# Keys through the DMA crossbar, and batch 0's queries split by token, in a fused pooling-attention and maxout feed-forward kernel

## Chip, cores, metric

One core of one Trainium2 chip. Times are device microseconds (us) of one execution, medians of the runs of a kernel; kernels that are compared ran on the same chip. Ratios are the mean time of one kernel's fast runs over that of the other's fast runs of the same rounds, so they are not quite the ratio of the medians that stand beside them.

## The reference

```python
# B, H, S, D = 8, 8, 576, 64; pool = 8, so 72 pooled keys and values per head
k_p, v_p = mean of k, v over groups of 8 tokens
attn = softmax(q @ k_p.T / 8)                  # 576 x 72 per head
x = (attn @ v_p), heads side by side           # 4608 tokens x 512
h = max(max(x @ w1, x @ w2), x @ w3)           # 4608 x 768
out = h @ w_out                                # 4608 x 512, float32
```

## The kernel before

The feed-forward runs in nine blocks of 512 tokens. In each block TensorE's stream is a list of groups: 18 hidden groups of four 512-column matmuls (six column slices of the hidden layer, three weights each), then 4 projections. Behind a group the plan puts pieces of the attention of the batch that comes next: `s0` to `s7` the scores of a head, `v0` to `v4` the values of a token chunk, `x0` to `x4` that chunk's transpose, `T` the next batch's query transpose, `k` its keys. Block 0 and all before it, the head, have a plan of their own.

Tiles lie in one of two on-chip memories: SBUF, into which the loads go, and PSUM, which TensorE writes its results to. The pooled keys of a batch lie as 96 rows of 6 x 128. They are transposed, and copied into a key matrix `kz` of two halves, one for even and one for odd token positions (`par`). The scores of every head need both halves.

```python
def keys(b, tag):                                   # six transposes on TensorE, into PSUM
    pkt = psp.tile([128, 6, 96], BF16, name="pkt", ...)
    for i in range(6):
        nc.tensor.transpose(pkt[:, i, :], kps[b][:, i, :, :], ident[0:96, 0:96])
    return pkt

def fill_kz(b, par, h0, h1, pkt, evac):
    rows = slice(64 * par, 64 * par + 64)
    evac(out=kz_all[b % 2][rows, par, h0:h1, 0:Sp].rearrange("p h (r i) -> p h r i", i=6),
         in_=pkt[rows, :, 12 * h0:12 * h1].rearrange("p i (h r) -> p h r i", r=12))

def turn_k(b):
    pkt = keys(b, TR)
    for par in range(2):
        fill_kz(b, par, 0, H, pkt, nc.scalar.copy if b == 1 else nc.vector.tensor_copy)
...
# head: loads of batch 0 in this order
load_k(0, ((2, 4), (4, 6)));  load_q(0, 0, 2);  load_q(0, 2, 4);  load_v(0, (0, 4, 6, 8))
...
def plan(n):                                        # blocks 1 to 8; a number is a group of the block
    b, i = n + 1, 3 * (n == 1)
    got = {0: [], 3: [], 3 + i: [(b, "k")]}
    got.update({5 + i + h: [(b, f"s{h}")] for h in range(H)})
    got[12 + i].append((b + 1, "T"))
    got.update({15 + i + c: [(b, f"v{c} x{c}")] for c in range(5)})
```

`fill_kz` copies from PSUM. How long one such copy takes (min/median/max, in ns, with the first and last start and the shapes):

```profile
L179 ACT COPY kz<-pkt x4: 393/513/634, 10.2 to 30.9; 64x288 bf16<-64x288 bf16 x2, 64x576 bf16<-64x576 bf16 x2
```

The softmax here doesn't subtract the row's maximum and nothing guards it: scores larger than these inputs give would overflow.

Of the kernel before, what the change touches and what calls it, by code (L numbers as in the profile page):

```python
# [14 lines left out]
def kernel(  # L15
# [11 lines left out]
    nc = tc.nc  # L27
# [11 lines left out]



    NG = 9
    GS = (0, 2, 4, 6, 8, 1, 3, 5, 7)
    NR = 64
    KCH = C // 128
    JCH = DFF // 128
# [8 lines left out]
    psp = ctx.enter_context(tc.tile_pool(name="psp", bufs=1, space=PSUM))  # L55
    ctx.enter_context(tc.manual_schedule())

    kts, vts, qbs, kps, qTs, ets = {}, {}, {}, {}, {}, {}

    def after(loads, first):  # L60
        for x in loads:
# [16 lines left out]
        for h, g in zip(cuts, cuts[1:]):  # L78
            nc.gpsimd.dma_start(out=vts[b][:, h:g], in_=src[:, h:g])  # L79

    def load_q(b, i=0, j=4):
        if b not in qbs:
            qbs[b] = ld.tile([128, 4, NG, D], BF16, name="qb", tag="qb")
        src = q[b].rearrange("h s d -> (h s d)").rearrange(
            "(hp p t d) -> p hp t d", hp=4, p=128, t=NG)
        nc.gpsimd.dma_start(out=qbs[b][:, i:j], in_=src[:, i:j])

    w_sb = [const.tile([128, KCH, DFF], F16, name=f"mw{wi}", tag=f"mw{wi}")
            for wi in range(3)]
# [9 lines left out]
    kt0 = const.tile([96, 2, POOL, D], F32, name="kt0", tag="kt0")  # L99
    nc.sync.dma_start(out=kt0, in_=rows_k(0)[:, 0:2])  # L100
    load_k(0, ((2, 4), (4, 6)))
    load_q(0, 0, 2)
    load_q(0, 2, 4)
    load_v(0, (0, 4, 6, 8))
    warm = const.tile([128, 512], BF16, name="warm", tag="warm")
    nc.vector.memset(warm, 1.0)
    ident = const.tile([128, 128], BF16, name="ident", tag="ident")
# [52 lines left out]
    def turn_q(b, n0, n1, evac, tag):  # L160
        if b not in qTs:
            qTs[b] = sb2.tile([128, 2 * NG, 128], BF16, name="qT", tag="qT")
        pqt = psp.tile([128, n1 - n0, 128], BF16, name="pqt", tag=tag[0],
                       bufs=tag[1])
        qf = qbs[b].rearrange("p hp t d -> p (hp t d)")
        for n in range(n0, n1):
            nc.tensor.transpose(pqt[:, n - n0, :], qf[:, 128 * n:128 * n + 128],  # L167
                                ident)
        evac(out=qTs[b][:, n0:n1, :], in_=pqt)

# [10 lines left out]
             in_=pkt[rows, :, 12 * h0:12 * h1].rearrange("p i (h r) -> p h r i", r=12))  # L181

    def turn_k(b):
        pkt = keys(b, TR)
        for par in range(2):
            fill_kz(b, par, 0, H, pkt,
                    nc.scalar.copy if b == 1 else nc.vector.tensor_copy)

    def pool_k(b, tag):

# [8 lines left out]
    def score(b, h, out, tp, i0, i1):  # L199

        f = NG * (h // 2) + tp
        n = f // 2
        nc.tensor.matmul(out, kz_all[b % 2][:, f % 2, h, :],  # L203
                         qTs[b][:, n + i0:n + i1, 64 * (h % 2):64 * (h % 2) + 64],
                         start=True, stop=True)

    def exp(out, in_):
# [45 lines left out]
    PW = ("pw", 3)  # L253

    QS = ((0, 5), (5, 10), (10, 14), (14, 18))
    xns, mms = {}, []

    def do(b, steps):




        for name in steps.split():
            i = int(name[1:] or 0)
            if name[0] in "qQ":
                turn_q(b, *QS[i], nc.vector.tensor_copy if name[0] == "Q"
                       else nc.scalar.copy, TR)
            elif name[0] == "T":
                qTs[b] = sb2.tile([128, 2 * NG, 128], BF16, name="qT", tag="qT")
                nc.sync.dma_start_transpose(  # L270
                    out=qTs[b], in_=qbs[b].rearrange("p hp t d -> p (hp t d)"))
            elif name[0] == "k":
                turn_k(b)
            elif name[0] == "K":
                pool_k(b, PW)
            elif name[0] == "a":
                nc.vector.tensor_tensor(out=k16, in0=kts[b][:, :, 0:4],
                                        in1=kts[b][:, :, 4:8], op=ALU.add)
            elif name[0] == "s":
                if i == 0:  # L280
                    new_et(b)
                scores(b, i)
            elif name[0] == "v":
                xns[b, i] = values(b, CHUNKS[i][0])
            else:
                turn_x(b, *CHUNKS[i], xns[b, i], TR,
                       nc.vector.tensor_copy if name[0] == "X" else nc.scalar.copy)

    def hidden_part(n, jc, c0, c1, hT):
        col = slice(NB * n + c0, NB * n + c1)  # L290
        t = None
        for wi in range(3):
            pw = psp.tile([128, c1 - c0], F32, name=f"pw{wi}", tag="pw", bufs=3)
            for kc in range(KCH):
                mm = nc.tensor.matmul(pw, w_sb[wi][:, kc, bass.ts(jc, 128)],  # L295
                                 xT[:, kc, col],
                                 start=(kc == 0), stop=(kc == KCH - 1))
            mms.append(mm)
            if wi == 0:
                t = sb2.tile([128, c1 - c0], F16, name="t0", tag="t0")  # L300
                nc.scalar.copy(out=t, in_=pw)  # L301
            elif wi == 1:
                t1 = sb2.tile([128, c1 - c0], F16, name="t1", tag="t1")
                nc.vector.tensor_tensor(out=t1, in0=t, in1=pw, op=ALU.max)  # L304
                t = t1
            else:
                nc.vector.tensor_tensor(out=hT[:, jc, c0:c1], in0=t, in1=pw,  # L307
                                        op=ALU.max)
            yield

    def hidden(n, hT):

        parts = [(0, JCH, 0, NB)]
        if n == 0:
            parts = [(0, 1, 0, 128), (0, 1, 128, 256), (1, 2, 0, 256), (0, 2, 256, NB),
                     (2, JCH, 0, NB)]
        elif n == 1:
            parts = [(0, 1, 0, 256), (0, 1, 256, NB), (1, JCH, 0, NB)]
        for j0, j1, c0, c1 in parts:
            for jc in range(j0, j1):  # L320
                yield from hidden_part(n, jc, c0, c1, hT)

    def project(n, hT):
        for mm in range(4):
# [3 lines left out]
            for c in ((slice(0, C // 2), slice(C // 2, C)) if last else (slice(0, C),)):  # L328
# [8 lines left out]
                for u in range(2):  # L337
                    b, g = divmod(2 * m + u, NG)
                    dst = out[S * b:S * b + S, :].rearrange("(r g) c -> r g c", g=NG)
                    (nc.scalar if last and u else nc.sync).dma_start(  # L340
                        out=dst[:, GS[g], c], in_=osb[64 * u:64 * u + 64, c])
            yield

    def new_hT():
# [5 lines left out]
    def heat(n):  # L350
        for _ in range(n):
            nc.tensor.matmul(wm, warm[:, 0:128], warm, start=True, stop=True)
# [6 lines left out]
    for i in range(0, 6, 2):  # L359
# [7 lines left out]
            out=kps[0][:, i:i + 2].rearrange("p i a d -> p a i d"),  # L367
            in0=f[:, None, :, 0].to_broadcast([96, 2, 2, D]),
            in1=f[:, None, :, 1].to_broadcast([96, 2, 2, D]), op=ALU.add)
    turn_q(0, 0, 5, nc.vector.tensor_copy, PW)  # L370
    turn_q(0, 5, 9, nc.scalar.copy, ATT)
    pkt0 = [keys(0, PW) for _ in range(2)]
    for h in (0, 4):
        fill_kz(0, 0, h, h + 4, pkt0[0], nc.vector.tensor_copy)
        fill_kz(0, 1, h, h + 4, pkt0[1], nc.scalar.copy)

    def scores4(h):
        psc = psp.tile([128, 4, 256], F32, name="psc4", tag="att", bufs=2)
        for i in range(4):
            score(0, h + i, psc[:, i, :], 0, 0, 4)  # L380
        exp(ets[0][:, h:h + 4, 0:256], psc[0:Sp])

    def scores2(h):
        psc = psp.tile([128, 2, 512], F32, name="psc2", tag="att", bufs=2)
        for i in range(2):
            score(0, h + i, psc[:, i, 0:64], 0, 4, 5)
            score(0, h + i, psc[:, i, 64:320], 1, 0, 4)
        exp(ets[0][:, h:h + 2, 256:S], psc[0:Sp, :, 0:320])

    def first_values():  # L390
# [11 lines left out]
                out=xns[0, 0][:, g], in0=pav[:, :, 0:D],  # L402
                in1=rcp.to_broadcast([128, 4, D]), op=ALU.mult)

    def first_turn(g, tag):
        pxt = psp.tile([128, 2, 128], F16, name="pxt0", tag=tag[0], bufs=tag[1])
        for kc in range(2):
            nc.tensor.transpose(pxt[:, kc, :],
                                xns[0, 0][:, g, 2 * kc:2 * kc + 2, :], identh)
        nc.scalar.copy(out=xT[:, 2 * g:2 * g + 2, 0:128], in_=pxt)  # L410

    scores4(0)
    heat(1)
    turn_q(0, 9, 14, nc.vector.tensor_copy, PW)
    turn_q(0, 14, 18, nc.vector.tensor_copy, PW)
    heat(2)
    scores4(4)
    pool_v(0, 0, 4, PW, nc.vector.tensor_copy)
    scores2(0)
    pool_v(0, 4, 6, PW, nc.vector.tensor_copy)  # L420
    pool_v(0, 6, 8, PW, nc.vector.tensor_copy)
    scores2(2)
    first_values()
    scores2(4)
    heat(1)
    first_turn(0, PW)
    xns[0, 1] = values(0, 128)
    first_turn(1, TR)
    scores2(6)


    def block(n, plan):
# [3 lines left out]
        for part in (hidden(n, hT), project(n, hT)):  # L436
            for _ in part:
# [6 lines left out]

    fold_v(1)
    fold_k(2, nc.gpsimd)
    block(0, {0: [(0, "X1")], 3: [(0, "v2")], 5: [(0, "v3")], 6: [(0, "x2")],
              8: [(0, "x3")], 10: [(0, "v4")], 12: [(0, "x4")],
              13: [(1, "a")], 15: [(1, "K")], 17: [(1, "k")], 19: [(1, "Q0")],
              20: [(1, "Q1")], 21: [(1, "Q2 s0")], 22: [(1, "Q3 s1")],  # L450
              23: [(1, "s2 s3")], 24: [(1, "s4 s5")], 25: [(1, "s6 s7")],
              26: [(1, "v0")], 27: [(1, "v1 x0"), (2, "T")], 28: [(1, "v2 x1")],
              29: [(1, "v3 x2")], 30: [(1, "v4")]})


    def plan(n):
# [1 line left out]
        got = {0: [], 3: [], 3 + i: [(b, "k")]}  # L458
        got.update({5 + i + h: [(b, f"s{h}")] for h in range(H)})
        got[12 + i].append((b + 1, "T"))  # L460
        got.update({15 + i + c: [(b, f"v{c} x{c}")] for c in range(5)})
        if n == 1:
            got[0].append((1, "x3"))
            got[3].append((1, "x4"))
# [46 lines left out]
```

## Time and profile before

| | before |
|---|---|
| median of the first 3 runs | 242.89 us (242.68 to 245.43) |
| span of the profiled run | 241.0 us |
| first scores / first feed-forward group / end of block 0 / last matmul's start | 10.34 / 16.96 / 48.69 / 236.25 us |

The last row is read from the starts of TensorE's instructions; it cuts the span into a head, the blocks and a tail. The prediction shows the page's first line, the busy time by stage and the timeline of the head.

### The profile page before, as it was taken

Reading aid. Unit: us, or ns where it says so; the run is one execution under the profiler, and the core shown is the slowest. Engines: PE = TensorE matmul, PEld = TensorE weight load, DVE = VectorE, ACT = ScalarE, POOL = GpSimd, SP = SyncE. Lnnn points to the kernel's source line nnn. Section 1 sums busy time; section 2 is a strip of 40 time slices with the busy share of each in tenths; the row PEclk is TensorE's granted clock in tenths of the full one; section 3 lists DMA queues with packets and bytes.
Section 4 is the critical chain, followed back from the end, with each engine's and each line's share of the span. In section 5 each row is a group of like instructions: output and inputs, shape, how many; then the busy total and the mean of one; then the engine's idle time right before and its main releaser. Section 6 shows DMA issues by size and latency. Waiting matters only on the chain.

```text
span 241.0 us, 4221 instructions
## 1 busy us (share of the span) xinstructions
PE 230.9 (96%) x1609; PEld 122.7 (51%) x1609; DVE 131.7 (55%) x239; ACT 100.1 (42%) x173; POOL 123.7 (51%) x91
## 2 busy tenths in 40 slices
PE   7698999999999999999999999999999999999992
PEld 3376555575554555455545554555455544444441
DVE  6856754665583558354836483648364834504530
ACT  2373247546513651365235523552355232142121
POOL 8864276989997479638880979286500000000000
PEclk9999999999999999999999999999999999999999
DMA  7999999999948995699769987997640253043006
GB/s 135 188 198 206 196 202 208 169 166 241 184 97 153 222 166 120 128 194 197 131 125 156 227 176 133 193 192 135 133 93 0 69 123 85 3 108 66 0 20 154
DMA packets 51939, 34.29 MB, mean 142 GB/s; under 512 B 32144, under 2 KB 46480, under 8 KB 51920
## 3 DMA queue, kind: packets, MB, share of 16 engines
q0 software_dynamic: 17088, 17.11, 45.5%
q1 hardware_dynamic: 34672, 16.79, 34.3%
q8 instruction: 12, 0.20, 0.3%
q10 hardware_dynamic: 160, 0.13, 0.2%
q14 instruction: 7, 0.06, 0.1%
HBM read 34.60 MB, written 9.44 MB: 183 GB/s over the span
## 4 chain that ended last, share of the span: by engine, by line
PE 89%; DVE 5%; ACT 2%; DMA 2%; issue 1%; DVEq 0%
PE pw L295 55%; PE po L331 19%; PE psc L203 6%; PE pav L238 4%; DMA kt<-in_k_dram 2%; PE pxt L229 1%; DVE kf L362 1%; ACT et L208 1%; DVE t L304 1%; PE pkt L174 1%; PE pvp L156 1%; DVE xn L246 1%; PE pqt L167 1%; DVE kp L366 1%; DVE kf L364 1%
## 5 line engine op out<-in xcount | busy, mean ns | idle before, releaser
L295 PE MATMUL pw<-xT,mw 128*128 128x512 f16 (+2 forms) x696 | 155.6, 364 | 0.8 <-ACT xT L233 0.7
L295 PEld LDWEIGHTS <-mw 128*128 128x128 f16 x696 | 61.8, 98 | 56.2 <-issue 1.0
L304 DVE TENSOR_TENSOR t<-t,pw 128x512 f16<-128x512 f16 (+2 forms) x58 | 37.8, 651 | 71.0 <-PE pw L295 43.7
L301 ACT CAST t<-pw 128x512 f16<-128x512 f32 (+2 forms) x58 | 32.3, 556 | 56.1 <-PE pw L295 54.8
L331 PE MATMUL po<-mwo,hT 128*128 128x512 f16 (+1 forms) x222 | 50.7, 373 | 0.0
L208 ACT ACTIVATE et<-psc 72x576 f16<-72x576 f32 (+2 forms) x62 | 40.7, 662 | 20.9 <-PE psc L203 20.7
L307 DVE TENSOR_TENSOR hT<-t,pw 128x512 f16<-128x512 f16 (+2 forms) x58 | 37.7, 650 | 9.0 <-PE pw L295 5.3
L336 ACT COPY osb<-po 128x512 f32<-128x512 f32 (+1 forms) x36 | 20.9, 580 | 47.7 <-PE po L331 43.7
L135 POOL TENSOR_TENSOR half<-vt 72x2048 f32<-72x2048 f16 x7 | 28.4, 4060 | 10.0 <-DMA vt<-in_v_dram 9.9
L331 PEld LDWEIGHTS <-hT 128*128 128x128 f16 x222 | 20.3, 97 | 21.3 <-DVE hT L307 2.4
L135 POOL TENSOR_TENSOR half<-kt 96x1536 f32<-96x1536 f16 x6 | 18.5, 3085 | 23.4 <-DMA kt<-in_k_dram 23.3
L246 DVE TENSOR_TENSOR xn<-pav,rcp 128x512 f16<-128x512 f32 x39 | 27.0, 691 | 1.5 <-DVE rcp L244 0.2
L136 POOL TENSOR_TENSOR half<-half 72x1024 f32<-72x1024 f32 (+1 forms) x13 | 27.2, 2096 | 1.0
L203 PE MATMUL psc<-qT,kz 128*128 128x64 bf16 (+3 forms) x192 | 25.9, 246 | 0.4 <-DVE kz L179 0.3
L203 PEld LDWEIGHTS <-kz 128*128 128x128 bf16 x192 | 17.8, 98 | 15.7 <-DVE kz L179 1.5
L238 PEld LDWEIGHTS <-et 72*128 72x128 f16 x312 | 15.2, 98 | 7.6
L238 PE MATMUL pav<-vp,et 72*128 72x65 f16 x312 | 16.5, 194 | 0.0
L244 DVE RECIPROCAL rcp<-pav 128x8 f32<-128x8 f32 x39 | 7.9, 204 | 9.4 <-PE pav L238 9.3
L139 POOL TENSOR_TENSOR kp<-half 96x384 bf16<-96x384 f32 x12 | 11.7, 993 | 0.5
L179 DVE COPY kz<-pkt 64x576 bf16<-64x576 bf16 (+1 forms) x14 | 9.9, 711 | 2.9 <-PE pkt L174 2.7
L79 POOL DMA_DIRECT2D vt<-in_v_dram x10 | 8.0, 804 | 2.9 <-DMA qb<-in_q_dram 2.2
L139 POOL TENSOR_TENSOR vp<-half 72x512 f16<-72x512 f32 x7 | 8.9, 1268 | 0.5
(48 smaller groups left out, 79.1 us busy)
## 6 DMA issues: line engine op xcount, KB each, us to landing
out_dram<-osb SPq DMA_DIRECT2D x70, 128.0 KB, 2.4
kt<-in_k_dram POOLq DMA_DIRECT2D x7, 576.0 KB, 7.4
qb<-in_q_dram POOLq DMA_DIRECT2D x7, 576.0 KB, 12.2
vt<-in_v_dram POOLq DMA_DIRECT2D x7, 576.0 KB, 15.0
mw<-in_moe_w_dram POOLq DMA_DIRECT2D x9, 256.0 KB, 9.3
mwo<-in_moe_w_out_dram POOLq DMA_DIRECT2D x1, 768.0 KB, 18.1
qb<-in_q_dram POOLq DMA_DIRECT2D x2, 288.0 KB, 7.0
xT<-xn SPq DMA_TRANSPOSE x30, 2.4
```

What stands on the lines that cost most here:

```text
L135: e.tensor_tensor(out=f, in0=t[:, :, 0:4, :], in1=t[:, :, 4:8, :], op=ALU.add)
L136: e.tensor_tensor(out=f[:, :, 0:2, :], in0=f[:, :, 0:2, :], in1=f[:, :, 2:4, :], op=ALU.add)
L203: nc.tensor.matmul(out, kz_all[b % 2][:, f % 2, h, :], qTs[b][:, n + i0:n + i1, 64 * (h % 2):64 * (h % 2) + 64], start=True, stop=True)
L208: nc.scalar.activation(out=out, in_=in_, func=FT.Exp, scale=1.0 / 64.0)
L238: nc.tensor.matmul(pav[:, h // 4, 65 * (h % 4):65 * (h % 4) + 65], ets[b][:, h, c0:c0 + 128], vp_all[:, b, h, :], start=True, stop=True)
L246: nc.vector.tensor_tensor(out=xn, in0=pv[:, :, :, 0:D], in1=rcp.to_broadcast([128, 2, 4, D]), op=ALU.mult)
L295: mm = nc.tensor.matmul(pw, w_sb[wi][:, kc, bass.ts(jc, 128)], xT[:, kc, col], start=(kc == 0), stop=(kc == KCH - 1))
L301: nc.scalar.copy(out=t, in_=pw)
L304: nc.vector.tensor_tensor(out=t1, in0=t, in1=pw, op=ALU.max)
L307: nc.vector.tensor_tensor(out=hT[:, jc, c0:c1], in0=t, in1=pw, op=ALU.max)
L331: nc.tensor.matmul(po, hT[:, jc, bass.ts(mm, 128)], wo_sb[:, jc, c], start=(jc == 0), stop=(jc == JCH - 1))
L336: nc.scalar.copy(out=osb[:, c], in_=po)
```

## The change

The intent: take the key transposes of batches 3 to 7 off TensorE (the crossbar of the DMA does them), and bring the first feed-forward group of the head forward. The load of batch 0's queries is split by token, so that values can be loaded after the first 256 tokens' queries; the feed-forward groups of the weight that is loaded last are held back. Cut to its core (left out: batch 0's tokens are taken in another order, and the heating matmuls, which multiply dummy data, `wm<-warm`, stand in other places):

```diff
 def turn_k(b):
-    pkt = keys(b, TR)
+    pkt = keys(b, TR) if b < 3 else kTs[b]
     for par in range(2):
-        fill_kz(b, par, 0, H, pkt, nc.scalar.copy if b == 1 else nc.vector.tensor_copy)
+        fill_kz(b, par, 0, H, pkt, nc.vector.tensor_copy if b == 2 else nc.scalar.copy)
...
+    elif name[0] == "Z":
+        kTs[b] = sb2.tile([128, 6, 96], BF16, name="kT", tag="kT")
+        nc.sync.dma_start_transpose(out=kTs[b], in_=kps[b].rearrange("p i a d -> p (i a d)"))
...                                                   # plan of blocks 1 to 8
-    got.update({15 + i + c: [(b, f"v{c} x{c}")] for c in range(5)})
+    got.update({14 + i + c: [(b, f"v{c} x{c}")] for c in range(5)})
+    got[17 + i].append((b + 1, "Z"))
...                                                   # loads of batch 0
-    load_q(0, 0, 2);  load_q(0, 2, 4);  load_v(0, (0, 4, 6, 8))
+    nc.gpsimd.dma_start(out=q0s[0], in_=rows_q(0)[:, :, 0:4])
+    load_v(0, (0, 4, 6, 8))
+    nc.gpsimd.dma_start(out=q0s[1], in_=rows_q(0)[:, :, 4:9])
...                                                   # head, after the scores of tokens 0 to 255
-    (query transposes, scores of the later tokens and pooled values in turn)
+    pool_v(0, 0, 4, ...); pool_v(0, 4, 6, ...); pool_v(0, 6, 8, ...)
+    first_values();  turn_q(0, 8, 13, nc.scalar.copy, PW)
+    first_turn(0, PW, nc.scalar.copy);  scores2(0)
+    xns[0, 1] = values(0, 128)
+    first_turn(1, TR, nc.vector.tensor_copy)
...                                                   # block 0: first two weights early, third after
+    early = [(0, 0, 128), (0, 128, 256), (1, 0, 256)] if n == 0 else []
+    for jc, c0, c1 in early: (groups of weights 0 and 1, result kept)
+    for jc, c0, c1 in early: (group of weight 2)
-    block(0, {0: [(0, "X1")], 3: [(0, "v2")], 5: [(0, "v3")], ...
+    block(0, {0: [(0, "S2 X1 r")], 1: [(0, "S4")], 3: [(0, "S6")], 6: [(0, "v2")], ...
...                                                   # outputs of the last two row blocks
-    (nc.scalar if last and u else nc.sync).dma_start(...)
+    e = nc.sync
+    if u and m >= TOK // 128 - 2:
+        e = nc.scalar if last else nc.gpsimd
+    e.dma_start(...)
```

## The prediction

> **What bounds the kernel now.** I read the page's first part (busy time by engine), then the busy time of each engine by stage, then TensorE's timeline of the first 30 us, VectorE's and ScalarE's beside it, the chain that ended last in one later block, and the last 5 us. The program has a head (batch 0's attention and the first block of 512 tokens, up to 48.7 us), eight more blocks, and a tail.
>
> ```profile
> PE 230.9 (96%) x1609; PEld 122.7 (51%) x1609; DVE 131.7 (55%) x239; ACT 100.1 (42%) x173; POOL 123.7 (51%) x91
> ```
> ```profile
> 8.90:17.00 8.10, 7.76 (x103) 6.06 (x104) 5.04 (x16) 5.70 (x10) 5.44 (x9) 1.00 1.36 197
> 17.00:27.00 10.00, 8.72 (x106) 6.71 (x104) 6.84 (x18) 3.85 (x10) 4.11 (x6) 1.00 1.25 205
> ...
> 73.40:97.90 24.50, 24.50 (x168) 12.59 (x167) 13.89 (x24) 10.73 (x18) 17.88 (x11) 1.00 0.88 159
> ```
> The columns of the second view are the stretch, its length, and the busy time of TensorE, its weight loads, VectorE, ScalarE and GpSimd. From the second block on TensorE is never idle at full clock: only TensorE work taken away helps there. In the head it is not full, and there a wait can be won or lost. A 512-column matmul takes 0.216 us from start to start; from that I count about 38 us of work between 8 and 52 us, and 5.5 us of gaps.
>
> TensorE's timeline, with its idle time and what ended it, shows where:
> ```profile
> 8.87 0.68 PE L167 MATMUL pqt<-ident,qb 128*128 128x128 bf16 x9 [2.07 <-DMA qb<-in_q_dram]
> 10.34 0.69 PE L203 MATMUL psc<-qT,kz 128*128 128x256 bf16 x4 [0.29 <-DVE kz L179]
> ...
> 14.98 0.49 PE L397 MATMUL pav<-vp,et 72*128 72x65 f16 x8
> ...
> 16.96 0.62 PE L295 MATMUL pw<-xT,mw 128*128 128x128 f16 x4
> ...
> 18.74 0.42 PE L238 MATMUL pav<-vp,et 72*128 72x65 f16 x8
> ...
> 21.62 0.40 PE L229 MATMUL pxt<-identh,xn 128*128 128x128 f16 x4 [0.16 <-DVE xn L246]
> 22.69 1.03 PE L295 MATMUL pw<-xT,mw 128*128 128x256 f16 x8 [0.67 <-ACT xT L233]
> ```
> First scores at 10.34, first values at 14.98, first feed-forward group at 16.96, batch 0's third values (tokens 256 to 383) at 18.74. Transfers are not quite the bound: from the records of the transfers, batch 0's values have landed at 12.2, and the first slices of the three weights at 13.6, 14.9 and 16.3; TensorE saw the first queries 1.1 us after their last packet (7.75 to 8.86).
>
> **What the Trainium skill says.** "TensorE: Matmul & The Clock Gate", section "Part 4: PE-mode transpose", gives about 275 ns for a 128x128 bf16 transpose in a kernel and says that the result lands in PSUM and needs a copy. This trace differs on the cost that counts: one record is 205 ns for 96x96, but six follow each other in 0.26 us. "DMA: Bandwidth & Descriptors", section "DMA Transpose (X-bar)", says that only the hardware queues do it, into SBUF, from 2-byte types and partitions in multiples of 16; the keys (96 partitions, bf16, issued by SyncE) fit, and the queries already go this way in this trace, 5.9 us from issue to landing for 576 KB. The same page, section "SWDGE vs HWDGE vs iDMA", says that GpSimd's transfers have software-made descriptors and those of SyncE and ScalarE hardware-made ones; here GpSimd's first transfer was issued at 1.27 and its first packet moved at 3.10, 1.8 us, against 2.4 us to full landing for an output from SyncE. This matters for the tail.
>
> **The change part by part.**
>
> *Keys of batches 3 to 7 by the crossbar.* The chain of a later block:
> ```profile
> 124.84 0.86 PE pw L295 x4
> 125.70 0.26 PE pkt L174 x6
> 125.96 1.73 PE pw L295 x8
> ```
> Six transposes stand in the full TensorE stream and cost 0.26 us. Five batches: **-1.3 us**. Added are five DMA transposes of 144 KB on SyncE. They are queued after the fourth attention chunk of the block before, some 95 us for the block that begins at 97.9; at the 2.4 us that a 128 KB transpose takes to land they are there by 98.5, and the copies into the key matrix stand four groups into the block, near 101.3. GpSimd's folded keys are ready at 88.5 in that block (last fold begun at 86.5, two of 0.99 us). So no wait. The two copies (0.63 us each on ScalarE, 0.76 before on VectorE) move to ScalarE, busy 10.7 of 24.5 us in such a block: hidden. Values begin one group earlier (14 instead of 15); the last exponential is two groups of 0.86 us ahead, against 0.65 for it: hidden.
>
> *Tail.* The last output's four parts: SyncE issues its last one late, because it has one issue of the row block before it to make (0.59 us).
> ```profile
> 236.38 1.43 SPq L340 DMA_DIRECT2D out_dram<-osb  x2
> 236.56 0.42 DVE L334 COPY osb<-po 128x256 f32<-128x256 f32 x1 [4.51 <-PE po L331]
> 237.02 0.51 ACTq L340 DMA_DIRECT2D out_dram<-osb  x1
> ```
> Its last issue runs from 237.90 to 238.45, though VectorE has the data at 236.98. With one issue given to GpSimd it starts near 237.1: 0.75 us earlier. GpSimd's own issue at 235.9 should move from about 237.7 and end near 238.6, about when SyncE's ends. I take **-0.6 us**.
>
> *Batch 0 in two parts, third weight late.* No TensorE work goes away (one more heating matmul, 0.2 us); only the order and the waits change. I lay the new order with the durations of the trace. Keys ready as before, scores of tokens 0 to 255 at 10.3 and 10.9, exponentials (1.02 us each) end at 12.0 and 13.0. Values pooled without the query transposes between: 11.55 to 13.3 (eight of 0.108, sixteen of 0.056). First values at 13.5, so **1.45 us earlier** than 14.98. Then transposes of the late queries at 13.9, whose copy is now on ScalarE (640 columns, 0.69 us, worked out from 0.59 for 512 and 0.37 for 256): 14.4 to 15.05; late scores at 15.1; values of tokens 128 to 255 at 15.4; VectorE's reciprocal (0.2) and product (0.7) end at 16.8; only after it, VectorE being in order, comes its copy of the second half of the first token chunk (about 0.28): 17.1. The first feed-forward group can start two of its four matmuls at 15.8 but **finishes at 17.2**, as before (17.4). Over a microsecond of TensorE is lost waiting for this copy.
>
> After that the remaining queries' transposes wait for the one PSUM buffer that the chunk's transpose fills (freed by VectorE at 18.35), and the scores of heads 4 and 5 wait for their copy (19.35). The last late exponential ends at 21.5, not 17.9, and the third values stand at 21.6, not 18.7. By 19.4 I count 3.1 us of gaps since 10.3, against 1.5 before: **+1.6 us**. What follows is milder, since more groups stand between: gaps before were 2.6 us from 19.4 to the block's end. Laid out the same way the new order has about as much (VectorE runs without a break from 22 to 26), plus 0.2 for the heating matmul. But groups moved ahead give slack that such a hand layout, which adds every latency, underrates. I discount the sum to **+1.3 us**. Holding the third weight's groups back gains nothing by itself, as the first two weights' slices were not awaited and the third lands at 16.3 plus 1.1, near when it is first wanted even in the old order.
>
> Sum: 242.9 - 1.3 - 0.6 + 1.3 = **242.3 us**.
>
> **The rivals.** (1) *The head gains.* First values come 1.45 us earlier, and if the stall at the first group is smaller than I have it, and the slack hides the later chains, up to 2 us of the 5.5 us of gaps go: 242.9 - 1.9 - 2 = 239 to 240. For it: the gaps at 21.6 and 22.7 are short chains that more distance would hide. Against: the exponentials of the late tokens now run beside the feed-forward copies, on ScalarE. (2) *The head loses in full.* My layout taken as it stands gives +2.3 or more: 243.3 to 244; for it, the single PSUM buffer and VectorE's unbroken run. (3) *The crossbar becomes a wait.* If the transposes queue behind the software transfers and land 3 us later than I have it, five blocks would wait: each us is 5 us in all, 246 or more. Against: queries of four times the size land in 5.9 us, and about 2.8 us of slack stand beside them. (4) *Weights bind.* The last slices land at 30.6 to 33.2; the old order used the first of them at 33.6. A head faster by over 2 us would meet them, which caps rival 1.
>
> **Range and chances.** Only the head is in doubt by more than half a microsecond: from -2 to +2.5 us around nothing gained, with 1.9 us sure elsewhere. So 240.3 to 244.2 eight times in ten. Faster by 2% needs 238.0, more than all gaps that the weights allow (0.04); slower by 2% needs 247.7, only by rival 3 (0.02).
>
> **What would show it.** Right: no key transposes after 77 us and each block from the third shorter by 0.26 us; the last output issue of SyncE near 0.75 us after TensorE's end instead of 1.4; first values near 13.5; the first group's third matmul at 17.1, waiting for VectorE's copy of xT; the query transposes waiting for VectorE; the third values after 21. Wrong: the first group complete by 16, or the first block's end (48.7 before) earlier than 48, or TensorE waiting for the key matrix's copy in a later block.

## More of the kernel before

One more view, the timeline of a later block (start, duration, engine, line, operation, what is made of what, shapes, count, and in brackets the idle time before and what ended it), shows how keys went into the scores:

```profile
76.90 0.42 PE L174 MATMUL pkt<-ident,kp 96*128 96x96 bf16 x6
77.15 1.89 PE L295 MATMUL pw<-xT,mw 128*128 128x512 f16 x8
...
77.36 1.54 DVE L179 COPY kz<-pkt 64x576 bf16<-64x576 bf16 x2 [0.43 <-PE pkt L174]
...
78.88 0.41 PE L203 MATMUL psc<-qT,kz 128*128 128x320 bf16 x3
```

VectorE's two copies are done at 78.90, and the scores start at 78.88: the fit is tight, with nothing to spare for a longer copy.

## The result

The changed kernel took **250.81 us** (249.90 to 251.84, 4 runs) against 243.05 us before (242.68 to 245.43, 4 runs): ratio 1.030, 95% interval 1.022 to 1.038, **slower by 3%**. The forecast was 242.3 us in a range of 240.3 to 244.2.

The same cuts through both profiled runs say where the 8.3 us of span come from (differences of the starts given above, and of the span):

| stretch | before | after | difference |
|---|---|---|---|
| start to first scores | 10.34 | 11.14 | +0.80 |
| first scores to end of block 0 | 38.34 | 40.09 | +1.75 |
| end of block 0 to last matmul | 187.56 | 193.09 | +5.53 |
| last matmul to end | 4.73 | 4.97 | +0.24 |

Most of it is in the blocks that were to gain 1.3 us. The busy time by stage of the changed kernel (as in the prediction: stretch, length, then TensorE, weight loads, VectorE, ScalarE, GpSimd, clock, DMA share, GB/s), for part of the head and for the block that answers to the block at 73.40 before:

```profile
17.00:27.00 10.00, 7.64 (x102) 6.46 (x100) 6.00 (x17) 4.60 (x10) 4.38 (x6) 1.00 1.26 205
75.98:101.37 25.39, 24.38 (x162) 12.21 (x161) 12.15 (x22) 13.04 (x20) 17.84 (x11) 1.00 0.92 162
```

That block is 25.4 us long, not 24.3 (from 73.61 to 97.88 in the chain before), and TensorE is idle for one of them. Its waits, in total, over the whole changed kernel (who waited for whom: us, times, longest):

```profile
PE psc L209 <- ACT kz L185: 4.4, 5, 0.9
...
PE pqt L172 <- DMA q<-in_q_dram: 1.4, 1, 1.4
PE pw L316 <- DVE xT L443: 1.0, 1, 1.0
PE pqt L172 <- DVE xT L247: 0.5, 1, 0.5
PE psc L217 <- DVE qT L175: 0.4, 1, 0.4
```

Five waits for ScalarE's copy into the key matrix, one in each block whose keys came by the crossbar; the others shown lie in the head. The timeline of that block answers to the one shown of before:

```profile
79.63 0.58 ACT L322 CAST t<-pw 128x512 f16<-128x512 f32 x1 [2.00 <-PE pw L316]
80.24 2.35 ACT L185 COPY kz<-kT 64x576 bf16<-64x576 bf16 x2
...
81.46 0.31 PE L209 MATMUL psc<-qT,kz 128*128 128x320 bf16 x1
...
82.65 0.29 PE L209 MATMUL psc<-qT,kz 128*128 128x192 bf16 x2 [0.87 <-ACT kz L185]
```

The two copies take 2.35 us, 1.16 each, where I had put 0.63. The first score waits for the first of them and the second for the second. From the starts of the matmuls I get gaps of 0.30 and 1.05 us; the brackets show less, because they count from a modelled end. That is 1.35 us per block in place of the 0.26 us of transposes: 5 x 1.09 = 5.45 of the 5.53 us. The crossbar itself was not late: from issue to landing it took 2.4 us in the median, as I had it, and 3.7 at most; by the trace's landing times each of the five landed at least 2.6 us before its copy began, and no wait names it.

The head went as laid out, including the waits. TensorE's timeline there:

```profile
14.70 0.55 PE L430 MATMUL pav<-vp,et 72*128 72x65 f16 x8
...
16.96 0.27 PE L316 MATMUL pw<-xT,mw 128*128 128x128 f16 x2
18.23 0.27 PE L316 MATMUL pw<-xT,mw 128*128 128x128 f16 x2 [1.00 <-DVE xT L443]
...
19.52 0.44 PE L172 MATMUL pqt<-ident,q 128*128 128x128 bf16 x5 [0.52 <-DVE xT L247]
...
20.54 0.44 PE L217 MATMUL psc<-qT,kz 128*128 128x192 bf16 x4 [0.36 <-DVE qT L175]
...
22.63 0.42 PE L252 MATMUL pav<-vp,et 72*128 72x65 f16 x8
```

From the starts, the three gaps shown are 1.16, 0.68 and 0.52 us. All of it is shifted by the 0.8 us of the late start. First values stand 3.56 us after the first scores (before 4.64); the first group starts 5.82 us after them (before 6.62) but stops in its middle; the third values come 11.49 us after them, before 8.40.

### The profile page after: what moved, and what is told of

It reads as the page before. It is cut to its first block, busy times and chain, and to the rows that moved or that the text cites. A ratio compares the mean times of both kernels' runs of the same rounds, so it can differ in the third digit from the quotient of the medians.

```text
span 249.3 us, 4216 instructions
## 1 busy us (share of the span) xinstructions
PE 233.2 (94%) x1600; PEld 123.1 (49%) x1600; DVE 122.3 (49%) x230; ACT 112.5 (45%) x185; POOL 124.2 (50%) x92
## 4 chain that ended last, share of the span: by engine, by line
PE 84%; ACT 8%; DMA 3%; DVE 2%; issue 1%; POOL 0%; DVEq 0%; POOLq 0%
PE pw L316 51%; PE po L359 19%; PE psc L209 6%; ACT kz L185 5%; PE pav L252 4%; DMA q<-in_q_dram 3%; ACT t L322 1%; PE pqt L172 1%; PE psc L217 1%; PE pxt L243 1%; PE pvp L160 1%; DVE xn L260 1%; POOL kt L73 0%; ACT xT L247 0%; PE pkp L200 0%
## 5 line engine op out<-in xcount | busy, mean ns | idle before, releaser
L316 PEld LDWEIGHTS <-mw 128*128 128x128 f16 x708 | 62.9, 98 | 55.2 <-issue 1.5
L327 DVE TENSOR_TENSOR t<-t,pw 128x512 f16<-128x512 f16 (+1 forms) x56 | 36.9, 658 | 93.9 <-PE pw L316 57.4
L359 PE MATMUL po<-mwo,hT 128*128 128x512 f16 (+1 forms) x222 | 49.7, 373 | 0.0
L330 DVE TENSOR_TENSOR hT<-t,pw 128x512 f16<-128x512 f16 (+1 forms) x56 | 36.9, 658 | 9.0 <-PE pw L316 5.5
L209 PE MATMUL psc<-qT,kz 128*128 128x320 bf16 x168 | 23.7, 247 | 5.1 <-ACT kz L185 4.4
L209 PEld LDWEIGHTS <-kz 128*128 128x128 bf16 x168 | 15.8, 98 | 21.7 <-ACT kz L185 8.6
L185 ACT COPY kz<-kT 64x576 bf16<-64x576 bf16 x10 | 11.6, 1162 | 0.2
L73 POOL DMA_DIRECT2D kt<-in_k_dram x9 | 5.0, 562 | 11.0 <-PE pw L316 6.5
L383 PE MATMUL wm<-warm 128*128 128x512 bf16 x22 | 8.7, 541 | 1.5 <-DVE warm L110 1.5
```

The costliest lines, as they stand in the source:

```text
L209: nc.tensor.matmul(out, kz_all[b % 2][:, f % 2, h, :], qTs[b][:, n + i0:n + i1, 64 * (h % 2):64 * (h % 2) + 64], start=True, stop=True)
L316: mm = nc.tensor.matmul(pw, w_sb[wi][:, kc, bass.ts(jc, 128)], xT[:, kc, col], start=(kc == 0), stop=(kc == KCH - 1))
L327: nc.vector.tensor_tensor(out=t1, in0=t, in1=pw, op=ALU.max)
L330: nc.vector.tensor_tensor(out=hT[:, jc, c0:c1], in0=t, in1=pw, op=ALU.max)
L359: nc.tensor.matmul(po, hT[:, jc, bass.ts(mm, 128)], wo_sb[:, jc, c], start=(jc == 0), stop=(jc == JCH - 1))
```

## The experiments

Nine edits start from the kernel before (e1, e2, e3, e5, e6, e9, e12, e13, e14), six from the changed kernel. "Head only" is the changed kernel with keys, copies, value slots and tail put back. Medians are in us and over all runs; those of e3, e10 and e14 include slow runs, and of e8 the two fast runs are given. The last column is the ratio of fast runs to those of the kernel before, with its 95% interval. e5 measures copies, not a time, and is not in the table.

| run | median | before | ratio |
|---|---|---|---|
| e1 keys by crossbar, copies on ScalarE | 248.46 | 242.88 | 1.023 (1.021 to 1.025) |
| e2 the same, copies on VectorE | 242.01 | 242.88 | 0.996 (0.994 to 0.998) |
| e3 as e1, other walk | 262.87; fast 259.35 and 261.40, 2 slow | 242.88 | 1.072 (1.066 to 1.077) |
| e4 head only | 244.60 | 242.88 | 1.007 (1.005 to 1.009) |
| e6 as e1, copies two groups earlier | 242.08 | 242.93 | 0.999 (0.994 to 1.004) |
| e7 head only, half chunk first | 244.62 | 242.93 | 1.009 (1.004 to 1.013) |
| e8 head only, third weight in order | 244.29 and 244.44 fast; 2 slow | 242.93 | 1.006 (1.003 to 1.008) |
| e9 as e2, copies two groups earlier | 245.21 | 242.93 | 1.008 (1.004 to 1.012) |
| e10 changed kernel, copies on VectorE | 244.02; 1 of 4 slow | 242.93 | 1.003 (0.999 to 1.007) |
| e11 e7 with the late queries elsewhere | 243.17 | 242.93 | 1.001 (0.997 to 1.006) |
| e12 tail only | 243.13 | 242.93 | 1.002 (0.998 to 1.006) |
| e13 as e1, one copy on each engine, values one group earlier | 242.58 | 242.99 | 0.999 (0.994 to 1.004) |
| e14 e6, values one group earlier | 241.80; 1 of 6 slow | 242.99 | 0.995 (0.990 to 1.000) |
| e15 changed kernel mended | 243.05 | 242.99 | 0.998 (0.994 to 1.003) |

Runs of one kernel spread by 2 us and more, the kernel before too (242.7 to 245.3 in e13 to e15). Over the 17 profiles TensorE saw the first queries between 8.2 and 10.4 us, with the old loads (8.2 to 10.4) as with the new (8.5 to 10.3). So I don't ascribe the 0.80 us of the first row to the change. For the same reason I read stages, not whole times, where a few tenths matter.

**e1: the keys alone.**
```diff
-    pkt = keys(b, TR)
+    pkt = keys(b, TR) if b < 3 else kTs[b]
-                    nc.scalar.copy if b == 1 else nc.vector.tensor_copy)
+                    nc.vector.tensor_copy if b == 2 else nc.scalar.copy)
+    (step "Z", and got[17 + i].append((b + 1, "Z")))
```

> Kernel before with only the keys of batches 3 to 7 by the crossbar and both copies into the key matrix on ScalarE. Theory A (the copies, 1.16 us each from SBUF, finish after the scores want them): five gaps of 1.3 us less five times 0.26 us of transposes, so +5.4 us, 248.3. Rival B (the loss of 7.8 us is the head's, the blocks only follow): -1.3 us, 241.6. Rival C (the added transfers slow the loads): some gain, gaps not at the copies.

248.46 us, +5.6. Theory A holds, B and C fall. The profile has the changed kernel's copies and its waits; the tile's view gives the copy's duration (min/median/max, in ns):
```profile
L179 ACT COPY kz<-kT x10: 1152/1163/1177, 77.5 to 180.6; 64x576 bf16<-64x576 bf16 x10
```

**e2: the same, copies on VectorE.**
```diff
-                    nc.vector.tensor_copy if b == 2 else nc.scalar.copy)
+                    nc.scalar.copy if b == 1 else nc.vector.tensor_copy)
```

> As e1, but the copies of batches 3 to 7 stay on VectorE. Theory A1 (ScalarE is slow at this copy, VectorE is not slower from SBUF than 0.76 us from PSUM): no gap, -1.3 us, 241.6. Theory A2 (the read from SBUF is slow on any engine, 1.1 us or more each): gap of about 1 us per block remains, 246 to 248.

242.01 us, -0.9: A1. One word separates +5.6 from -0.9. The copy from SBUF is shorter on VectorE than the one from PSUM was (0.75 us):
```profile
L179 DVE COPY kz<-kT x10: 631/643/1274, 77.0 to 175.6; 64x576 bf16<-64x576 bf16 x10
```
The full 1.3 us was not reached: its median gains 0.9. In its profiled run (243.05, the slowest of its four) the blocks gain nothing, 187.58 us from the end of block 0 to the last matmul; one gap of 0.75 us and one of 0.2 stand where a block waits to begin, and one copy came late, after a key transpose that took 4.1 us to land. Gaps at a block's start are also in the profiles of e1 (0.4), e3 (0.4), e5 (1.3) and e10 (1.6, put down by the profile to a token chunk's transpose), all with key transposes on the crossbar, but not in those of the changed kernel, e6, e9 and e13 to e15, which have them too. The profiles without key transposes on the crossbar (before, e4, e7, e11, e12) show none; a slow run of e8 does (0.8). So the added transfers may delay a token chunk now and then, a milder form of rival 3. No run tests it.

**e3: the same elements, another walk.**
```diff
+    order = "p h i r" if b > 2 else "p h r i"
-    ... "p h (r i) -> p h r i" ... "p i (h r) -> p h r i"
+    ... f"p h (r i) -> {order}" ... f"p i (h r) -> {order}"
```

> As e1, copies on ScalarE, the same elements walked in another order: contiguous reads of SBUF (12 in a row) and writes 12 bytes apart, where e1 reads 192 bytes apart and writes contiguously. If strided 2-byte reads of SBUF make the 1.16 us, the copy falls to about 0.63 us and the gaps to at most 0.3 us: 241.6 to 243. If it is reading SBUF at all (not PSUM) by ScalarE, it stays 1.16 us and 248.

Neither: the copy went to 2.12 us and the kernel to 259.35 and 261.40 us in its two fast runs (the other two were slow). Reading in order did not help, because now the writes were 12 bytes apart. My alternative had left out that a write's stride may cost more than a read's. So the walks were measured one at a time.

**e5: copies by themselves.** Only their durations count (one look, at a lower clock of TensorE, 258.72 us).
```diff
+    flat, turned = s.rearrange("p i q -> p (i q)"), s.rearrange("p i q -> p q i")   # s: the crossbar's tile
+    for _ in range(3):
+        e(out=o[:, 0, 0:576], in_=flat)                                          # in order, in order
+        e(out=o[:, 1, 0:576].rearrange("p (q i) -> p q i", i=6), in_=turned)     # read 192 B apart
+        e(out=o[:, 2, 0:576].rearrange("p (q i) -> p i q", i=6), in_=s)          # written 12 B apart
+        fill_kz(7, 0, 0, H, kTs[7], e)                                           # the real one
```

> Kernel e2 with copies measured by themselves before the last block, three of each kind on ScalarE and then on VectorE, 64x576 bf16 from the crossbar's tile in SBUF into SBUF: both sides in order; read 192 bytes apart and written in order; read in order and written 12 bytes apart; and the real copy into the key matrix. If the read's stride costs on ScalarE, the four take about 0.63, 1.16, 2.1, 1.16 us; if any read from SBUF costs, the first takes 1.1 us as well. On VectorE the real one is 0.64 us (e2). Time is of no interest (some 10 us more).

The tile's view, in ns, in the order of the edit for VectorE and then ScalarE:
```profile
L495 DVE COPY side<-kT x3: 293/294/299, 211.7 to 232.9; 64x576 bf16<-64x576 bf16 x3
L496 DVE COPY side<-kT x3: 628/630/633, 212.0 to 233.1; 64x576 bf16<-64x576 bf16 x3
L497 DVE COPY side<-kT x3: 1118/1121/1123, 212.5 to 233.6; 64x576 bf16<-64x576 bf16 x3
L495 ACT COPY side<-kT x3: 670/670/670, 216.8 to 225.6; 64x576 bf16<-64x576 bf16 x3
L496 ACT COPY side<-kT x3: 1152/1152/1163, 217.4 to 226.2; 64x576 bf16<-64x576 bf16 x3
L497 ACT COPY side<-kT x3: 2107/2107/2107, 218.4 to 227.2; 64x576 bf16<-64x576 bf16 x3
```
The expectation for ScalarE was met. On ScalarE, reading SBUF costs next to nothing by itself (0.67 us in order, against 0.63 for the real copy from PSUM); reading it 192 bytes apart costs 0.48 us more, writing 12 bytes apart 1.44 more. In ScalarE's copies from PSUM the same 192-byte walk was free: 0.63 us for 576 columns, where in-order ones of queries took 0.59 for 512 and 0.69 for 640. For VectorE it was not: 0.75 us, against 0.42 and 0.49 for those.

**e6: copies on ScalarE, two groups earlier.**
```diff
-    got = {0: [], 3: [], 3 + i: [(b, "k")]}
+    got = {0: [], 3: [], 1 + i: [], 3 + i: []}
+    got[(3 if b < 3 else 1) + i].append((b, "k"))
```

> As e1 (crossbar, copies on ScalarE), with the two copies placed two groups earlier in the block, after the second group and not the fourth. Theory A (the copies are late by the 1.35 us that TensorE waits, and 1.73 us earlier is enough): gaps gone, 241.6 to 242.2. Rival (ScalarE, in order, then delays the next feed-forward copy, or the crossbar's result is not there yet): gaps of 0.5 us or more remain, 244 to 247.

242.08 us, and no gap at the scores in the five blocks: from the end of block 0 to the last matmul it is 186.16 us, 1.40 less than before. The copies are as long as in e1, but nobody waits for them. The whole time alone (four runs from 241.44 to 243.92) did not settle the gain.

**e4: the head alone.** The edit is the diff above without keys, copies, value slots and tail.

> The changed kernel with its keys, copies, value slots and tail as before; only batch 0's split queries, their load order, the late third weight and block 0's plan are left. Theory: +2.5 us, 245.4, as the end of the first block moved from 48.7 to 51.2 us in the trace. Rival B: +7 or more. First queries seen 0.8 us later than before (9.7 against 8.9) if that belongs to the smaller rows; by chance, it is near 8.9 here and the loss is 1.7.

244.60 us, +1.7, with the first queries seen at 8.5. From first scores to the end of block 0 it takes 39.99 us (before 38.34, +1.65), and the gaps are the changed kernel's.

**e7: the half chunk first.**
```diff
     scores2(0)
+    first_turn(1, TR, nc.vector.tensor_copy)
     xns[0, 1] = values(0, 128)
-    first_turn(1, TR, nc.vector.tensor_copy)
```

> e4 (head only) with one swap: the second half of the first token chunk is transposed and copied before the values of tokens 128 to 255, not after. Theory (the 1.16 us gap at the first group is VectorE's order): the gap falls below 0.3 us; the later chain of X1 and the late queries then starts about 0.3 us later, so in all -0.5 to -0.9 us against e4, 243.7 to 244.1. Rival (the gap only moves to the next wait): no change, 244.6.

244.62 us, as e4: the rival holds. The gap of 1.16 us at the first group is gone, but one of 0.34 before the next chunk's transpose appears and the 0.68 and 0.52 stay. (Its profiled run started late, at the first queries 10.3, with a granted clock of 0.75 from 12 to 17 us, so its stages are not compared.) Mending the biggest wait in the list alone gained nothing.

**e11: e7, with the late queries elsewhere.**
```diff
-    turn_q(0, 13, 18, nc.vector.tensor_copy, TR)        # the one buffer that X1 also uses
+    turn_q(0, 13, 18, nc.vector.tensor_copy, PW)
-    block(0, {0: [(0, "S2 X1 r")], ...
+    block(0, {0: [(0, "S2 r X1")], ...
```

> e7 (head only, second half of the chunk first) with the late queries transposed into one of the three other PSUM buffers and ahead of the next token chunk. Theory (the waits of 0.68 and 0.52 us for the single buffer and for VectorE's copy are what is left of the head's loss): 243.2 to 243.8. Rival (VectorE and ScalarE carry the same work, any wait removed comes back at the next): 244.3 to 244.7, as e4 and e7.

243.17 us: the theory holds. With both waits gone and the order swapped, the head is level with the old one (1.001), not better. In e15, the same head with an ordinary start, the stretch from first scores to the end of block 0 is 38.36 us (before 38.34); e11's own profiled run, which saw its first queries late, at 9.97, has 38.93.

**e8: the third weight in order.**
```diff
-    early = [(0, 0, 128), (0, 128, 256), (1, 0, 256)] if n == 0 else []
+    early = []
-        parts = [(2, 3, 0, 256), (0, 3, 256, NB), (3, JCH, 0, NB)]
+        parts = [(0, 1, 0, 128), (0, 1, 128, 256), (1, 3, 0, 256), (0, 3, 256, NB), (3, JCH, 0, NB)]
```

> e4 (head only) with the third weight's groups in their old place after the second's, same 30 groups and same plan. If holding the third weight back gains nothing, the time is within 0.4 us of e4, 244.2 to 245.0; if it is what saves the head from waiting for weights, the first third group waits for its slice and the time is 0.5 to 1.5 us above e4; if it is part of the loss, below.

Two runs fell in the slow state; the two fast ones, 244.29 and 244.44, lie within e4's (244.18 to 244.83). Holding the third weight back neither gains nor loses that can be seen.

**e12: the tail alone.**
```diff
-    (nc.scalar if last and u else nc.sync).dma_start(
+    e = nc.sync
+    if u and m >= TOK // 128 - 2:
+        e = nc.scalar if last else nc.gpsimd
+    e.dma_start(
```

> Kernel before with only the tail: the second half of the last but one row block's output issued by GpSimd. The prediction said -0.6 us. From the trace of the changed kernel (SyncE waited 1.2 us at the end for GpSimd's transfer, 3.1 us after its issue) I now expect 0 to +0.3 us.

243.13 us, ratio 1.002: no gain. SyncE's last issue did come earlier: it starts 0.54 us after TensorE's end in the changed kernel and in e12, 1.37 after it in the kernel before. But the last transfers then take longer to land. The kernel before, then the changed kernel (number, KB each, median us from issue to landing):
```profile
out_dram<-osb ACTq DMA_DIRECT2D x2, 64.0 KB, 2.2
out_dram<-osb SPq DMA_DIRECT2D x2, 64.0 KB, 2.3
```
```profile
out_dram<-osb POOLq DMA_DIRECT2D x1, 128.0 KB, 3.1
out_dram<-osb ACTq DMA_DIRECT2D x2, 64.0 KB, 3.0
out_dram<-osb SPq DMA_DIRECT2D x2, 64.0 KB, 3.1
```
By the trace's landing times SyncE's last transfer is the last to land in each of these kernels: 3.45 us after TensorE's end in the kernel before, 3.46 in the changed one, 3.50 in e12. GpSimd issues at 244.19 in the changed kernel, and SyncE's longest wait at the end is for that transfer (1.3 us, where the kernel before waits 0.4 at most for an output):
```profile
244.19 0.56 POOL L371 DMA_DIRECT2D out_dram<-osb  x1 [66.61 <-ACT osb L364]
```
```profile
SPq L538 <- DMA out_dram<-osb: 1.7, 2, 1.3
```
Yet it lands at 247.3, before ScalarE's last (247.9) and SyncE's last (248.0): it is not what ends last. Why all of the last transfers take longer was not tested.

**e10: the changed kernel, copies on VectorE.** The edit is e2's, on the changed kernel.

> The changed kernel with one word changed: the copies of batches 3 to 7 on VectorE. If the loss is the sum of two parts that don't touch each other (copies on ScalarE +6.4 us, e1 less e2; head +1.7, e4), the time is 250.8 - 6.4 = 244.4 or less. If the parts share a cause, it is clearly above 245.5 or below 243.

244.02 us over all four runs; the three fast ones lie between 243.23 and 244.73. The parts add: the engine of the copies is worth 2.7% here (1.030 less 1.003, fast runs) and 2.7% between e1 and e2 (1.023 less 0.996).

**e9: copies on VectorE, two groups earlier.** The edits of e2 and e6 together.

> Candidate for the best: kernel before, keys of batches 3 to 7 by the crossbar, copies on VectorE (0.64 us each) and two groups earlier, so neither a late landing (e2's one wait of 0.7 us) nor the copies are waited for. Theory: -1.3 us, 241.6, in all five gaps; a late first landing may add some tenths. Rival (the copies hold up VectorE's work of the first groups, which were close): 242.5.

245.21 us: the rival holds, more strongly than I had it. With the copies behind the second group, VectorE clears the feed-forward's PSUM buffers later, and TensorE waits for that five times, some 0.4 us each from the starts:
```profile
PE pw L299 <- DVE hT L311: 1.2, 5, 0.3
```
From the end of block 0 to the last matmul it takes 188.30 us, 0.74 more than before. The medians differ by more, 2.3 us; the profiled run also saw its first queries late (10.14), and its head took 39.42 us, so the rest is not put down to the copies. So "earlier" is right for ScalarE and wrong for VectorE.

**e13: one copy on each engine, in the old place.**
```diff
-                    nc.vector.tensor_copy if b == 2 else nc.scalar.copy)
+                    nc.vector.tensor_copy if b == 2 or (b > 2 and par) else nc.scalar.copy)
+    (and the value slots at 14 + i + c, as in the changed kernel)
```

> Kernel before, keys of batches 3 to 7 by the crossbar in the old place, one copy on each engine (1.16 us on ScalarE, 0.64 on VectorE, side by side), values one group earlier as in the changed kernel. If the forecast's own mechanism holds once the copies fit, there is no gap before the scores: -1.3 us, 241.6. If the five blocks keep 0.2 us gaps or more elsewhere, 242 to 243.

242.58 us, the second of the two forecasts; the blocks take 187.13 us, 0.43 less than before. Small waits for ScalarE's 1.16 us remain at the scores' weight loads.

**e14: e6, values one group earlier.** The edit is e6's with the changed kernel's `14 + i + c`.

> e6 (both copies on ScalarE, two groups earlier) with values one group earlier, against late landings of the token chunks. As e6's trace had no gap in the five blocks: 241.6 (-1.3). If e6's spread of 2.5 us came from waits for the token chunks, the spread shrinks here; if from the landing of the first queries, it stays.

241.80 us, ratio 0.995 (0.990 to 1.000): the lowest median of all, 1.2 us below the kernel before, with the interval just below one, and not told apart from e2 or e6. Its blocks take 186.18 us, 1.38 less than before, as e6's, five times 0.28. Four runs lie between 241.3 and 241.9; two longer ones remain (244.2, and a slow 246.5), so moving the values did not remove the spread. TensorE's timeline in the block shown twice above has no gap:
```profile
73.20 5.34 PE L299 MATMUL pw<-xT,mw 128*128 128x512 f16 x24
78.38 0.41 PE L203 MATMUL psc<-qT,kz 128*128 128x320 bf16 x3
78.63 1.03 PE L299 MATMUL pw<-xT,mw 128*128 128x512 f16 x4
```

**e15: the changed kernel mended.** The changed kernel with e6's place for the copies, e11's head and the old tail.

> The changed kernel with its three losses mended: copies on ScalarE two groups earlier (e6), head as in e11, tail as before. If the parts add: the head of e11 (+0.2 to +0.3) and e6's -0.9 to -1.3 give 241.8 to 242.4; if the mended head hinders the blocks, 243 or more.

243.05 us, not the 241.8 to 242.4 of the sum. Its head is level (38.36 us), but its blocks take 187.43 us: in one block, at 175 us, ScalarE's copies began late, waiting for the crossbar, and TensorE lost 0.68 and 0.49 us. Two groups earlier leaves little room for a late key transpose; e14's ScalarE met two such waits too, at no cost. How often this happens is open.

## Why the prediction was wrong, point by point

**Keys by the crossbar: the step that failed.** The prediction said: "The two copies (0.63 us each on ScalarE, 0.76 before on VectorE) move to ScalarE, busy 10.7 of 24.5 us in such a block: hidden." The 0.63 us was measured on a copy that read PSUM; the crossbar writes to SBUF, and the same walk from there takes 1.16 us (e1, e5). And "hidden" was argued from ScalarE's share of busy time, not from when the scores need the copies. ScalarE is free for them at 80.24, after a feed-forward copy; TensorE, whose last matmul before the scores started at 80.94, could have begun them at about 81.16. Two copies of 0.63 would have ended at 81.5, so by this estimate even the duration I used did not quite fit. The term was -1.3 us; it measured +5.6 (e1).

**The rest of that step** was right. Without the transposes and without the wait the blocks are 1.38 to 1.40 us shorter (e6, e14), against 1.3 forecast. Landing in 2.4 us was right in the median, and values one group earlier were hidden (no wait in e14).

**Rival 3** said that each us of waiting in the five blocks costs 5 us, 246 or more. That arithmetic is what happened; the cause it named, late transfers, was not. The prediction's own list of signs ("TensorE waiting for the key matrix's copy in a later block") names the failure.

**The head** was forecast at +1.3 us; e4 measures +1.7. The waits came where they had been laid: 1.16 us at the first group ("over a microsecond"), then the late queries' transposes behind VectorE's copy (0.68) and the scores behind theirs (0.52); third values stand 11.49 us after the first scores, 11.3 in the layout. The layout's parts add up to 1.8 us (1.6 and 0.2 for the heating matmul), close to the 1.7 measured; the "+2.3 or more" of rival 2 does not follow from them. So the step was right and the discount to 1.3 was the error, of 0.4 us. The claim that the third weight's delay gains nothing held (e8).

**The tail** was forecast at -0.6; e12 shows +0.2, not to be told from nothing, and no gain. The issue came earlier as forecast (0.83 us, 0.75 forecast). The step that failed is that an issue 0.75 us earlier would end 0.75 us earlier: SyncE's last transfer took 2.92 us to land instead of 2.08, and so landed as late after TensorE's end as before (3.46 and 3.45 us). GpSimd's transfer took 3.1 us, where I had allowed 2.7, but was not the last. Why the transfers took longer stays open.

Sum of the parts by themselves: 5.6 + 1.7 + 0.2 = 7.5 us, against 7.8 measured. The miss of 8.5 us is 6.9 from the keys, 0.8 from the tail, 0.4 from the head, and some tenths of runs.

## What to carry to other kernels

When the step that makes some data is moved, the cost of the step that reads them can change: ask where that step now reads from and with what stride, and take its duration from an instruction of that form, or measure one, before calling it hidden. An engine that is busy under half of the time still delays everything if its work is due within a microsecond: compare the time at which it can start plus the duration with the time of need. A transfer issued earlier need not land earlier (e12). And of several chained waits, removing the largest may give nothing (e7) until the ones behind it are gone too (e11).

## What the Trainium skill lacked or had wrong

- "Advanced Engine Details and Errata", section "SBUF Cachelines", which I had not looked up, says that a different 16-byte line at each access brings a penalty and that the stride that is free depends on the type. It would have warned me. It gives no size: here, 64x576 bf16 in SBUF, 192-byte reads took ScalarE 1.15 us instead of 0.67 (e5). VectorE took 0.63 instead of 0.29, but no run here tells whether that has the same cause.
- The same section does not tell reads from writes. Writes 12 bytes apart cost far more than reads 192 bytes apart: 2.11 against 1.15 us on ScalarE, 1.12 against 0.63 on VectorE (e5).
- The same page, section "PSUM Cachelines", warns of non-contiguous patterns for matmuls. For ScalarE's copy out of PSUM, 192-byte steps in bf16 cost nothing that shows: 0.63 us for 576 columns, between 0.59 for 512 and 0.69 for 640 in order. VectorE's took 0.75, against 0.42 and 0.49. I found neither on any page.
- "TensorE: Matmul & The Clock Gate", section "Part 4: PE-mode transpose", gives some 275 ns per transpose in a kernel, for 128x128. That is the time of one record (here 0.21 us, for 96x96), not its cost in a full stream, which the section does not give: six cost 0.26 us together (chain before), and removing them gave 0.28 us per block (e6).
- No page that I read says that a first transfer's landing varies from run to run of one kernel: first queries were seen between 8.2 and 10.4 us.
